# Causal attention and two gated layers in one kernel: the first batch's maxima over v emitted beside the first step, ordered behind its scores' minimum on VectorE

## The chip, the cores and the metric

The kernel runs on one core of a Trainium2 chip. The metric is the device time of one launch in microseconds (us); lower is better. Engines are TensorE (PE in the profile), VectorE (DVE), ScalarE (ACT), GpSimd (POOL) and SyncE (SP), which here only issues transfers.

## The reference

q, k, v have 4 batches, 8 heads, 576 positions and a head size of 64; s has one value for each position of each head.

```python
scores = scale * q @ k.T
cum = cumsum(maximum(s, 0), axis=-1)
bias = -(cum[..., :, None] - cum[..., None, :])
scores = where(causal, -1e9, scores + minimum(bias, 0))
attn = exp(scores - max(scores))
attn = attn / (sum(attn) + 1e-9)
x = (attn @ v) as 2304 tokens x 512
h = x @ w_in;   g = h * tanh(softplus(h));       x = g @ w_out      # 512 x 2048, 2048 x 512
h = x @ w_in2;  g = h * sigmoid(1.702 * h);      out = g @ w_out2   # 512 x 2048, 2048 x 512
```

q, k, v, s are float32; the four weight matrices are float64 and are turned into pairs of float32 parts on the chip.

## The kernel before

**Attention in steps.** A tile is 128 query rows of one batch (i = 0 to 4, the last with 64 rows); a group is a tile with four of the eight heads (g = 0, 1). A group is worked in one step (first tile), two steps (second tile) or more. Step t emits: `do_qk` (scores `s` on TensorE from `qw` and `kw`, into one of 4 PSUM banks of the pool `ps_s`), `do_max` (line 346, on VectorE: scores plus the row `ck` of running sums, with the minimum `mx`; the scores carry the opposite sign, so this minimum is the reference's maximum), `do_exp` (ScalarE), `do_hilo` (a scaled 16-bit part on ScalarE, line 372, the remainder on VectorE, line 373, both in `hl`, then one transposing load `pt` issued by SP, line 377). Four steps later (LAG = 4) `do_av` multiplies `pt` with v (lines 397 and 401, into `o`), and line 406 adds the parts.

**What feeds a step.** `load_group` fetches `kraw`, `qraw`, `vraw` of a group (`vraw` has three buffers); line 166 transposes k and q on TensorE into `kt` and `qt`; lines 174, 175, 188 and 189 split them into two parts each (`kw`, `qw`). `v1` and `v2` (lines 198, 202) split v into two 16-bit parts, scaled by `vs`, one number for a batch. `vs` comes from the largest absolute value of the batch's v: `vscale_load` fetches the whole v in three pieces `vl` of 128 x 768 (line 218), reduces each on VectorE (line 219) and joins them (line 222); `vscale_set` spreads the result (line 227), transposes it on TensorE (`vx`, line 229) and takes the reciprocal (lines 231 to 236). For the first batch `vscale_load(0)` is called in the setup, before `queue_prep(0)`, and `vscale_set(0)` by the first `v1` inside the first `tick`. For batches 1 to 3 both are queued at the second-last and last tile of the batch before.

**Buffers.** The pieces `vl` take buffers of the pool `mo_a` (five, tag `hs`), which the weights in conversion (`wst`) and the first layer's outputs (`hs`) use too.

**Order.** A planner gives every engine its instruction order: it plays the program through with its own durations, and an engine takes, of the instructions that are ready in that plan, the one that the program emitted first. The order is then fixed for each engine, and on the chip an engine waits at an instruction whose inputs are late. `add_manual_dep` with `order` adds an edge to the plan without a semaphore of its own. SP's transfers are issued in a fixed order as well.

**After the first two tiles** the first layer (`first_layer`, lines 581 to 583) runs among the attention's steps, as soon as 256 tokens are done; later the rest of both layers follows on TensorE.

Of the kernel before, what the change touches and what calls it, by code (L numbers as in the profile page):

```python
# [9 lines left out]
F32 = mybir.dt.float32  # L10
# [4 lines left out]
ALU = mybir.AluOpType  # L15
# [36 lines left out]
def attention_moe_moe_kernel(  # L52
# [12 lines left out]
    nc = tc.nc  # L65
# [41 lines left out]
    order = mybir.DependencyInfo(mybir.DependencyClass.NoSync, mybir.DependencyReason.DATA)  # L107
# [20 lines left out]
    def tmp_pair(dt, nm):  # L128
        tmp_n[0] += 1
        p = mo_a if mo_b[0] is None or tmp_n[0] % (MA + MBB) < MA else mo_b[0]  # L130
        return p.tile([128, 1024], dt, tag="hs", name=nm)
# [78 lines left out]
    VC = 3  # L210
    VW = H * S * D // 128 // VC

    def vscale_load(b):
        flat = v[b].rearrange("h t d -> (h t d)").rearrange("(p n) -> p n", p=128)
        vmx[b] = m = sm_p.tile([128, VC + 1], F32, tag="vm", name="vm")
        for c in range(VC):
            t = tmp_pair(F32, "vl")[:, 0:VW]
            nc.sync.dma_start(out=t, in_=flat[:, c * VW:(c + 1) * VW])
            nc.vector.tensor_reduce(
                out=m[:, c:c + 1], in_=t, axis=mybir.AxisListType.X, op=ALU.max, apply_absolute_value=True  # L220
            )
        nc.vector.tensor_reduce(out=m[:, VC:VC + 1], in_=m[:, 0:VC], axis=mybir.AxisListType.X, op=ALU.max)

    def vscale_set(b):
        m = vmx.pop(b)
# [25 lines left out]
    def load_ck(b, g):  # L251
        t = ck_p.tile([128, HG * LK], F32, tag=f"ck{g}", name=f"ck{g}").rearrange("p (h t) -> p h t", t=LK)
        ck[b, g] = t
        load_ck_part(b, g, 0, 128)
        if b:
            load_ck_part(b, g, 128, LK)
# [7 lines left out]
    def load_ckp(b, g):  # L264
        t = ck_p.tile([128, HG * LK], F32, tag=f"ck{g}", name=f"cp{g}")
        t = t[:, 0:HG // 2 * S].rearrange("p (h t) -> p h t", t=S)
        for a in range(2):
            h0 = g * HG + 2 * a
            nc.sync.dma_start(
                out=t[64 * a:64 * a + 64], in_=cum_d[b:b + 1, h0:h0 + 2, :].to_broadcast([64, 2, S])  # L270
            )
        ckp[b, g] = t
# [38 lines left out]
    def segs(x):  # L311
        if len(x["hs"][0]) == 1:
            return [(0, x["L"])]
        m = x["L"] // 2
        return [(0, m), (m, x["L"])]

    def do_qk(x):
        b, i, g, n, L = x["b"], x["i"], x["g"], x["n"], x["L"]
        x["S"] = []
        for c0, c1 in segs(x):  # L320
            ps = ps_s.tile([128, 512], F32, tag="s", name="s")
            x["S"].append(ps)
            for e, hs in enumerate(x["hs"]):
                o = ps[:, e * L:e * L + c1 - c0]
                for a, h in enumerate(hs):
                    hl = h - g * HG
                    for w in range(2):
                        nc.tensor.matmul(  # L328
                            out=o, lhsT=qw[b, i, g][:, hl, w, :], rhs=kw[b, g][:, hl, c0:c1],
                            start=(e == a == w == 0), stop=False, skip_group_check=True,  # L330
                        )
                if c1 == L:
                    nc.tensor.matmul(  # L333
                        out=o[:, c1 - c0 - n:c1 - c0], lhsT=identb, rhs=maskb if n == 128 else maskp,
                        start=False, stop=True, skip_group_check=True,
                    )

    def do_max(x):
        b, i, g, L = x["b"], x["i"], x["g"], x["L"]
        mx = sm_p.tile([128, HG], F32, tag="mx", name="mx")  # L340
        x["P"] = p = pp.tile([128, S], F32, tag="P", name="P", bufs=PB)
        for e, hs in enumerate(x["hs"]):
            hl = hs[0] - g * HG
            c = ckp[b, g][:, hl] if len(hs) == 2 else ck[b, g][:, hl]
            for f, (c0, c1) in enumerate(segs(x)):
                nc.vector.tensor_tensor_reduce(  # L346
                    out=p[:, e * L + c0:e * L + c1], in0=x["S"][f][:, e * L:e * L + c1 - c0], in1=c[:, c0:c1],
                    scale=1.0, scalar=mx[:, e:e + 1] if f else 3.0e38, op0=ALU.add, op1=ALU.min,
                    accum_out=mx[:, e:e + 1],
                )  # L350
        x["mx"] = mx

    def do_exp(x):
        ts = tile_state(x)
        L, p = x["L"], x["P"]
        for e in range(x["mu"]):
            o = p[:, e * L:(e + 1) * L]
            lut(
                o, o, AF.Exp, bias=x["mx"][:, e:e + 1], scale=-1.0,
                accum_out=ts["sums"][:, x["j"] + e, 0:1],  # L360
            )

    def do_hilo(x):
        L, mu, nb = x["L"], x["mu"], x["nb"]
        Lp = nb * 128
        w = mu * Lp
        hl = pp.tile([128, 2 * NTIL * 128], F16, tag="hl", name="hl", bufs=HLB)
        hv = hl[:, 0:2 * w].rearrange("p (a w) -> p a w", a=2)
        if Lp != L:
            nc.gpsimd.memset(hv[:, :, L:Lp], 0.0)  # L370
        wl = mu * L
        nc.scalar.activation(out=hv[:, 0, 0:wl], in_=x["P"][:, 0:wl], func=AF.Copy, scale=PSC)  # L372
        nc.vector.scalar_tensor_tensor(  # L373
            out=hv[:, 1, 0:wl], in0=x["P"][:, 0:wl], scalar=PSC, in1=hv[:, 0, 0:wl], op0=ALU.mult, op1=ALU.subtract
        )
        x["T"] = d = pt_p.tile([128, 2 * NTIL, 128], F16, tag="pt", name="pt")
        last_pt[0] = nc.sync.dma_start_transpose(out=d[:, 0:2 * mu * nb, :], in_=hl[:, 0:2 * w])
# [71 lines left out]
    late_k = {}  # L449

    VSTEP = {(3, 0): vscale_load, (4, 0): vscale_set}

    def queue_prep(gi):
        if gi >= len(groups):
            return
        b, i, g = groups[gi]
        items, vs, kT = split_items(b, i, g)
        if 0 < gi < len(groups) - 1:
            prep_q.append(lambda: load_group(*groups[gi + 1]))
        if i == 0 and b > 0:  # L460
            late_k[groups.index((b - 1, NTIL - 1, g))] = kT
        else:
            items = items + [kT]
        if gi < 2:
            v_first.extend(vs)
        else:
            items = items + vs
        if b + 1 < B and (i, g) in VSTEP:
            items = items + [lambda: VSTEP[i, g](b + 1)]
        prep_q.extend(items)  # L470

    def pop_prep(m):
        for _ in range(min(m, len(prep_q))):
            prep_q.pop(0)()
# [6 lines left out]
    def tick():  # L481
        t = nxt[0]
        nxt[0] += 1
        if t < NS:
            x = steps[t]
            gi = x["gi"]
            if first_of[gi] == t:
                pop_prep(len(prep_q))
                queue_prep(gi + 2)
            left = last_of[gi] - t + 1  # L490
            npop = -(-len(prep_q) // left)
        else:
            npop = len(prep_q)
        if t < NS:
            do_qk(x)
            do_max(x)
            do_exp(x)
            if last_of[gi] == t and gi in late_k:
                late_k.pop(gi)()
            if last_of[gi] == t and x["i"] == LK // 128 - 1:  # L500
                load_ckp(x["b"], x["g"])
            if last_of[gi] == t and x["i"] == NTIL - 1 and x["b"] + 1 < B:
                load_ck(x["b"] + 1, x["g"])
            do_hilo(x)
        if t == VT:
            for f in v_first:
                f()
        pop_prep(npop)
        while avn[0] < NS and t - avn[0] >= LAG:
            x = steps[avn[0]]  # L510
            do_av(x)
            if x["last"]:
                norm_tile(x)
                emit_q.append((t + (1 if avn[0] < ES else EDEL), x))
            avn[0] += 1
        while emit_q and emit_q[0][0] <= t:
            emit_tile(emit_q.pop(0)[1])
# [67 lines left out]
    def l1_mm(ps, lay, m, xr, first):  # L585
# [15 lines left out]
        out=maskb, in_=maskb, pattern=[[-1, 128]], compare_op=ALU.is_ge, fill=BIG, base=0, channel_multiplier=1  # L601
    )
    nc.gpsimd.memset(maskp, 0.0)
    for a in range(2):
        nc.gpsimd.affine_select(
            out=maskp[64 * a:64 * a + 64], in_=maskp[64 * a:64 * a + 64], pattern=[[-1, 64]],
# [138 lines left out]
    for m in range(NF):  # L745
        if m % 2 == 0:
            t = tmp_pair(F32, "hs")
# [5 lines left out]
        if m % 2:  # L753
            nc.sync.dma_start(
                out=h_d[:, m - 1:m + 1, (NU - UE) * U:NT], in_=t.rearrange("p (m t) -> p m t", m=2)
# [11 lines left out]
    for i, (u, t0, W, m0, n) in enumerate(groups1):  # L767
# [9 lines left out]
        for j in range(n):  # L777
            m = m0 + j
# [9 lines left out]
        if m0 + n == NF:  # L788
            k_ = 512 // W
            for e in range(KC * W // 512):  # L790
# [4 lines left out]
                for p in range(2):  # L795
                    nc.sync.dma_start(
                        out=x2_d[:, p, cs, t0:t0 + W],
                        in_=x2[:, p].bitcast(F32).rearrange("p (c t) -> p c t", c=k_),
# [105 lines left out]
```

## Time and profile before

| | |
|---|---|
| median of 3 runs | 1068.95 us (1063.43 to 1071.94) |
| profiled execution | 1066.92 us, of which the span is 1065.1 us |
| TensorE busy | 999.0 us, 94% of the span |
| VectorE busy | 557.4 us, 52% |
| ScalarE busy | 484.5 us, 45% |
| GpSimd busy | 273.3 us, 26% |

The span runs from the first to the last instruction; 1.8 us of the profiled execution lie outside it. Durations in the rows are those of this one execution. A transfer's issue on SP is not its landing; the time from the one to the other stands in the rows on transfers.

### The profile page before, as it was taken

To read this page: it belongs to the slowest core of one execution; us is meant where nothing else is said; L and a number is where in the kernel's file an instruction comes from. 1 tells how busy PE (TensorE), PEld (TensorE's weight loads), DVE (VectorE), ACT (ScalarE), POOL (GpSimd) and SP (SyncE) were. 2 spreads that over 40 slices of the span, in tenths; PEclk is the share of its full clock that TensorE was granted. 3 is DMA by queue.
4 is the path that set the end of the run, shared out by engine and by line. 5 is a ranking of instruction groups with operands and counts; after the bars stand their busy time and mean duration, and the time that the engine had idled before them with its cause. 6 is when DMAs were issued, how large, how long until landed. Compare 5 with 4: busy or idle time off the path is not lost.

```text
span 1065.1 us, 16948 instructions
## 1 busy us (share of the span) xinstructions
PE 999.0 (94%) x6396; PEld 865.6 (81%) x6396; DVE 557.4 (52%) x1074; ACT 484.5 (45%) x1010; POOL 273.3 (26%) x307
## 2 busy tenths in 40 slices
PE   3688899989999999999999979899999999999998
PEld 3577798888989889987888869688888888888897
DVE  5798786674557863576534575662222222222231
ACT  4778777584658862463212343442222222222121
POOL 3445532341124112655232254220000100100000
PEclk7679899989999999999999989899999999999999
DMA  9899987996699796797533656520300300210010
GB/s 231 161 251 277 258 208 172 231 188 161 139 222 219 146 196 198 251 382 276 178 119 119 194 166 195 158 80 6 114 1 0 99 20 1 60 40 1 20 40 20
DMA packets 192562, 154.35 MB, mean 145 GB/s; under 512 B 117921, under 2 KB 161953, under 8 KB 192481
## 3 DMA queue, kind: packets, MB, share of 16 engines
q1 hardware_dynamic: 182240, 131.25, 46.6%
q0 software_dynamic: 10240, 22.03, 8.1%
q8 instruction: 50, 0.82, 0.3%
q14 instruction: 32, 0.25, 0.1%
HBM read 93.92 MB, written 33.10 MB: 119 GB/s over the span
## 4 chain that ended last, share of the span: by engine, by line
PE 55%; DMA 10%; DVE 5%; POOL 3%; issue 2%; ACT 2%; SPq 0%; ACTq 0%; POOLq 0%; DVEq 0%
PE acc L844 18%; PE h L581 9%; PE h L582 9%; PE h L583 9%; DMA wst<-in_moe_w_out_dram 3%; DMA wst<-in_moe_w_in_dram 2%; POOL w L577 2%; PE s L328 2%; DVE wst L570 2%; PE acc L583 2%; PE acc L582 2%; PE acc L581 2%; DMA hg<-h_d 2%; DVE wst L566 1%; PE o L397 1%
## 5 line engine op out<-in xcount | busy, mean ns | idle before, releaser
L581 PE MATMUL h<-xh,w 128*128 128x256 f32 (+1 forms) x768 | 252.5, 331 | 8.5 <-DVE z L831 5.1
L582 PE MATMUL h<-xh,w 128*128 128x256 f32 (+1 forms) x768 | 248.4, 324 | 0.0
L583 PE MATMUL h<-xh,w 128*128 128x256 f32 (+1 forms) x768 | 246.9, 322 | 0.0
L844 PE MATMUL acc<-w,gh 128*128 128x512 f32 x576 | 177.8, 390 | 0.0
L581 PEld LDWEIGHTS h<-xh,w 128*128 128x128 f32 x768 | 147.6, 193 | 21.3 <-DVE z L831 5.5
L582 PEld LDWEIGHTS h<-xh,w 128*128 128x128 f32 x768 | 148.1, 193 | 10.8
L583 PEld LDWEIGHTS h<-xh,w 128*128 128x128 f32 x768 | 147.5, 192 | 10.5 <-POOL w L577 0.2
L831 DVE TENSOR_TENSOR z<-h,sg 128x512 f32<-128x512 f32 x72 | 49.7, 690 | 193.1 <-ACT sg L112 192.7
L112 ACT ACTIVATE sg<-h 128x512 f32<-128x512 f32 x72 | 42.9, 596 | 204.2 <-PE h L583 204.2
L844 PEld LDWEIGHTS acc<-w,gh 128*128 128x128 f32 x576 | 107.6, 188 | 21.7
L582 PE MATMUL acc<-gl,w 128*128 128x512 f32 (+1 forms) x320 | 120.1, 375 | 4.0 <-DVE gl L717 4.0
L581 PE MATMUL acc<-gh,w 128*128 128x512 f32 (+1 forms) x320 | 119.7, 374 | 3.1 <-POOL w L574 1.7
L577 POOL TENSOR_TENSOR w<-wst,w 128x512 fp32r<-128x512 f32 x64 | 90.6, 1418 | 116.7 <-ACT w L576 115.6
L583 PE MATMUL acc<-gh,w 128*128 128x512 f32 (+1 forms) x320 | 117.6, 374 | 0.7 <-POOL w L577 0.7
L844 PE MATMUL acc<-w,gl 128*128 128x512 f32 x288 | 112.2, 389 | 0.0
L112 ACT ACTIVATE P<-P,mx 128x128 f32<-128x128 f32 (+4 forms) x144 | 83.4, 580 | 33.0 <-DVE mx L346 32.1
L328 PE MATMUL s<-kw,qw 128*128 128x288 f32 (+4 forms) x384 | 90.0, 347 | 7.3 <-DVE kw L175 3.7
L373 DVE SCALAR_TENSOR_TENSOR hl<-P,hl 128x512 f16<-128x512 f32 (+2 forms) x104 | 73.1, 703 | 29.7 <-ACT hl L372 29.4
L809 POOL DMA_DIRECT2D xh<-x_d x20 | 14.5, 727 | 284.2 <-PE h L583 196.2
L833 DVE TENSOR_TENSOR gl<-z,gh 128x512 fp32r<-128x512 f32 x72 | 50.4, 701 | 49.4 <-ACT gh L832 34.9
L346 DVE CUSTOM_DVE_ANT_0 P<-s,ck 128x128 f32<-128x128 f32 (+3 forms) x128 | 59.3, 485 | 31.7 <-PE s L333 30.6
L582 PEld LDWEIGHTS acc<-gl,w 128*128 128x128 f32 x320 | 61.4, 192 | 15.1 <-DVE gl L717 4.8
(90 smaller groups left out, 1723.7 us busy)
## 6 DMA issues: line engine op xcount, KB each, us to landing
h_d<-hs SPq DMA_DIRECT2D x36, 512.0 KB, 4.6
hg<-h_d SPq DMA_DIRECT2D x36, 512.0 KB, 6.4
wst<-in_moe_w_in_dram SPq DMA_DIRECT2D x32, 512.0 KB, 4.8
wst<-in_moe_w_out_dram SPq DMA_DIRECT2D x32, 512.0 KB, 3.9
x_d<-x SPq DMA_DIRECT2D x36, 256.0 KB, 2.4
xh<-x_d POOLq DMA_DIRECT2D x16, 512.0 KB, 5.5
vl<-in_v_dram SPq DMA_DIRECT2D x12, 384.0 KB, 5.4
cp<-cum_d SPq DMA_DIRECT2D x16, 288.0 KB, 5.1
```

What stands on the lines that cost most here:

```text
L112: i = nc.scalar.activation(out=out, in_=in_, func=func, **kw)
L328: nc.tensor.matmul(out=o, lhsT=qw[b, i, g][:, hl, w, :], rhs=kw[b, g][:, hl, c0:c1], start=(e == a == w == 0), stop=False, skip_group_chec ...
L346: nc.vector.tensor_tensor_reduce(out=p[:, e * L + c0:e * L + c1], in0=x["S"][f][:, e * L:e * L + c1 - c0], in1=c[:, c0:c1], scale=1.0, sca ...
L373: nc.vector.scalar_tensor_tensor(out=hv[:, 1, 0:wl], in0=x["P"][:, 0:wl], scalar=PSC, in1=hv[:, 0, 0:wl], op0=ALU.mult, op1=ALU.subtract)
L570: nc.vector.scalar_tensor_tensor(out=yi, in0=yi, scalar=-(2 ** 31), in1=zi, op0=ALU.bitwise_and, op1=ALU.bitwise_or)
L577: nc.gpsimd.tensor_tensor(out=tl_, in0=y, in1=th, op=ALU.subtract)
L581: nc.tensor.matmul(out=outp, lhsT=hi_w, rhs=hi_x, start=start, stop=False, skip_group_check=True)
L582: nc.tensor.matmul(out=outp, lhsT=hi_w, rhs=lo_x, start=False, stop=False, skip_group_check=True)
L583: nc.tensor.matmul(out=outp, lhsT=lo_w, rhs=hi_x, start=False, stop=stop, skip_group_check=True)
L831: nc.vector.tensor_tensor(out=z, in0=ps, in1=sg, op=ALU.mult)
L833: nc.vector.tensor_tensor(out=gl, in0=z, in1=gh, op=ALU.subtract)
L844: nc.tensor.matmul(out=acc[tb], lhsT=gx[:, ts], rhs=w[:, wx, :], start=m == 0 and a == 0, stop=m == NF - 1 and a == 2, skip_group_check=True,)
```

## The change

`vscale_load` now takes its three buffers and asks for its three loads first, and puts the four reductions into a function `maxima`. For batches 1 to 3 it calls that at once. For the first batch it stores it in `v_late`, and the first `tick` calls it (VT = 0) after `do_hilo` of step 0 and before `v1` and `v2`; each of the three large reductions gets an order edge behind the last minimum instruction of step 0. The loads stay where they were. No instruction is added or removed.

```diff
     def vscale_load(b):
         flat = v[b].rearrange("h t d -> (h t d)").rearrange("(p n) -> p n", p=128)
         vmx[b] = m = sm_p.tile([128, VC + 1], F32, tag="vm", name="vm")
+        ts = [tmp_pair(F32, "vl")[:, 0:VW] for _ in range(VC)]
         for c in range(VC):
-            t = tmp_pair(F32, "vl")[:, 0:VW]
-            nc.sync.dma_start(out=t, in_=flat[:, c * VW:(c + 1) * VW])
-            nc.vector.tensor_reduce(
-                out=m[:, c:c + 1], in_=t, axis=mybir.AxisListType.X, op=ALU.max, apply_absolute_value=True
-            )
-        nc.vector.tensor_reduce(out=m[:, VC:VC + 1], in_=m[:, 0:VC], axis=mybir.AxisListType.X, op=ALU.max)
+            nc.sync.dma_start(out=ts[c], in_=flat[:, c * VW:(c + 1) * VW])
+
+        def maxima():
+            for c in range(VC):
+                r = nc.vector.tensor_reduce(
+                    out=m[:, c:c + 1], in_=ts[c], axis=mybir.AxisListType.X, op=ALU.max, apply_absolute_value=True
+                )
+                if b == 0:
+                    tc.add_manual_dep(r.ins, max_last[0].ins.name, order, reason="behind the first scores")
+            nc.vector.tensor_reduce(out=m[:, VC:VC + 1], in_=m[:, 0:VC], axis=mybir.AxisListType.X, op=ALU.max)
+
+        if b == 0:
+            v_late.append(maxima)
+        else:
+            maxima()
@@
+    max_last, v_late = [], []
+
     def do_max(x):
@@
-                nc.vector.tensor_tensor_reduce(
+                last = nc.vector.tensor_tensor_reduce(
@@
         x["mx"] = mx
+        max_last.append(last)
@@
         if t == VT:
+            v_late.pop()()
             for f in v_first:
                 f()
```

## Rows read from the trace of the kernel before

**Rows 1.** Busy time by stretch: TensorE, its loads, VectorE, ScalarE, GpSimd; granted clock; DMA share.
```profile
0.00:60.80 60.80, 31.51 (x194) 26.72 (x194) 43.15 (x105) 37.29 (x98) 26.34 (x45) 0.71 0.91 202
60.80:133.00 72.20, 62.83 (x535) 54.71 (x535) 61.46 (x148) 58.35 (x141) 38.87 (x43) 0.89 1.06 265
133.00:400.00 267.00, 257.04 (x2468) 234.88 (x2467) 177.38 (x470) 186.14 (x467) 71.26 (x100) 0.98 0.87 188
```

**Rows 2.** VectorE in order of time: start, duration, line, operation, idle time before it.
```profile
9.40 0.95 DVE L219 TENSOR_REDUCE vm<-vl 128x1 f32<-128x768 f32 x1 [0.88 <-DMA vl<-in_v_dram]
...
12.06 0.69 DVE L175 TENSOR_TENSOR kw<-kt,kw 64x512 fp32r<-64x512 f32 x1
12.78 0.95 DVE L219 TENSOR_REDUCE vm<-vl 128x1 f32<-128x768 f32 x1
13.76 0.29 DVE L346 CUSTOM_DVE_ANT_0 P<-s,ck 128x128 f32<-128x128 f32 x1
...
14.61 0.15 DVE L222 TENSOR_REDUCE vm<-vm 128x1 f32<-128x3 f32 x1
...
16.39 0.15 DVE L236 TENSOR_SCALAR vs<-vs 128x1 f32<-128x1 f32 x1
16.46 0.68 DVE L373 SCALAR_TENSOR_TENSOR hl<-P,hl 128x512 f16<-128x512 f32 x1
17.06 1.27 DVE L202 SCALAR_TENSOR_TENSOR v<-vraw,vs,v 128x256 f16<-128x256 f32 x3
```

**Rows 3.** Transfers issued in short stretches: bytes each and median us from issue to landing.
```profile
ck<-cum_d SPq DMA_DIRECT2D x1, 256.0 KB, 5.7
...
pt<-hl SPq DMA_TRANSPOSE x1, 9.0
```

**Rows 4.** ScalarE in order of time, columns as in rows 2.
```profile
14.10 0.40 ACT L112 ACTIVATE P<-P,mx 128x128 f32<-128x128 f32 x1 [4.60 <-DVE mx L346]
...
15.78 0.63 ACT L372 ACTIVATE hl<-P 128x512 f16<-128x512 f32 x1
...
26.44 0.51 ACT L198 ACTIVATE v<-vraw,vs 128x256 f16<-128x256 f32 x1 [3.36 <-DMA vraw<-in_v_dram]
27.99 0.60 ACT L188 ACTIVATE qw<-qt 128x512 fp32r<-128x512 f32 x1 [1.05 <-PE qt L166]
```

**Rows 5.** SP's issues in order of time: start and time taken to issue.
```profile
7.56 1.33 SPq L259 DMA_DIRECT2D ck<-cum_d  x2
17.17 4.11 SPq L377 DMA_TRANSPOSE pt<-hl  x1
21.38 0.52 SPq L142 DMA_DIRECT2D vraw<-in_v_dram  x1
```

**Rows 6.** TensorE in order of time, columns as in rows 2.
```profile
15.19 0.45 PE L229 MATMUL vx<-ident,vw 128*128 128x128 f32 x1 [5.07 <-DVE vw L227]
15.43 1.06 PE L166 MATMUL qt<-ident,qraw 128*128 128x128 f32 x4
...
26.23 0.29 PE L397 MATMUL o<-v,pt 128*128 128x128 f16 x1 [6.86 <-DMA pt<-hl]
26.86 1.10 PE L166 MATMUL qt<-ident,qraw 128*128 128x128 f32 x4
...
60.79 0.79 PE L581 MATMUL h<-xh,w 128*128 128x256 f32 x2 [0.85 <-ACT xh L442]
```

**Rows 7.** Busy time by stretch around the first transposed load, columns as in rows 1.
```profile
17.20:21.30 4.10, 2.17 (x13) 2.03 (x12) 3.36 (x13) 2.74 (x11) 2.85 (x4) 0.77 1.16 335
21.30:26.20 4.90, 0.00 (x0) 0.00 (x0) 1.31 (x3) 1.72 (x5) 0.80 (x2) 0.63 1.15 179
```

**Rows 8.** GpSimd in order of time: the copy of the fourth group's q.
```profile
22.29 0.40 POOL L148 COPY qraw<-qraw 128x256 f32<-128x256 f32 x1
```

**Rows 9.** Waits between 246 and 266 us: engine, line, released by, us in total, times, longest.
```profile
PE qt L166 <- DVE mx L346: 2.3, 1, 2.3
...
DVE vm L219 <- DMA vl<-in_v_dram: 2.4, 1, 2.4
```

## The prediction

> **What bounds the kernel now.** Read first the busy times by stretch [rows 1]. TensorE is the bound of the whole, but not of the place that is changed. In the first 60.8 us it works 31.5 us, so 29.3 us are idle there; from 60.8 to 133 us it idles 9.4 us, from 133 to 400 us 10.0 us. The first stretch is a chain of latencies that ends where the first layer starts, at 60.79 us [rows 6]. What is won or lost on that chain moves all that follows. What is won beside it is worth nothing.
>
> Next read VectorE, ScalarE, SP and TensorE side by side from 9 to 30 us. VectorE takes the three large reductions between the splits of q and k, the last of them from 12.78 us, and starts the first minimum at 13.76 us, straight behind it [rows 2]. That looks like a wait for a reduction, but the minimum needs the row `ck` as well: its first load was issued at 7.56 us [rows 5] and landed 5.7 us later [rows 3], at 13.26 us. So the reduction holds the minimum for at most about half a microsecond. ScalarE has stood idle for 4.60 us when the minimum comes [rows 4], so this half microsecond is on the path there. From there the path goes through four exponentials, the scaled part (15.78 to 16.41 us) [rows 4], the remainder on VectorE at 16.46 us [rows 2] and the transposing load at 17.17 us [rows 5].
>
> That load is where the path is decided. It lands 9.0 us after its issue [rows 3], and TensorE, which has run out of other work in its order, waits 6.86 us for it, to 26.23 us [rows 6]. ScalarE waits at the same time for the fourth group's v, up to 26.44 us [rows 4], which SP issued at 21.38 us, behind the 4.11 us that the issue of the transposing load took [rows 5]. In those 9 us the mean share of the 16 DMA engines is 1.16 and 1.15 [rows 7]: they have a backlog.
>
> **The change part by part.** Removed ahead of the first minimum: three reductions of 0.95 us. Without them VectorE has only the second group's splits of q and k there (that of k took 0.69 us) [rows 2], and these no longer queue behind a reduction. `ck` becomes the last to come. The minimum then starts at about 13.30 us (13.26 plus the 0.03 to 0.04 us that lay between neighbours before) in place of 13.76: 0.46 us earlier. The other bound is 0, if the planner leaves something else there.
>
> Added behind it: the three reductions, 0.98 us from the start of one to what followed it (12.78 to 13.76) [rows 2], 2.94 us together. The small join began at 14.61 us [rows 2]; now it begins at 14.61 - 0.46 + 2.94 = 17.09 us, 2.48 us later, and so do the spreading, the transpose `vx` on TensorE, the reciprocal and the split of v.
>
> Who waits for that? The split of v on VectorE began at 17.06 us and took 1.27 us for three groups [rows 2]; it would be 19.54 us, and 20.0 us when the first group's v is split. Its product comes at 26.23 us, and the buffer that it frees is wanted by SP only at 21.38 us [rows 5]. That covers it with 1.4 us to spare; without the long issue of 4.11 us SP would wait for v here.
>
> The remainder of step 0 is the second one that can be held. It becomes ready at 16.46 - 0.46 = 16.00 us. The reductions would occupy VectorE from 14.15 to 17.09 us, the third from 16.11 us. If the planner puts the remainder ahead of the third, the transposing load is issued at 16.71 us, 0.46 us earlier; if it comes behind all three, it starts at 17.09, 0.63 us later than now. No row shows which. I take the first, since the program emits the remainder ahead of the reductions, and keep -0.46 and +0.63 as bounds.
>
> TensorE: `vx` stood right ahead of the third group's transposes (15.19 and 15.43 us) [rows 6]. Were the order kept, these and step 1's scores would slip by 2.48 us, to 17.9 us. Behind them TensorE idles 6.86 us [rows 6], which covers it. If `vx` is planned behind them, nothing slips.
>
> The loads for v stay in place. For batches 1 to 3 the same seven operations are emitted in another order, loads first. How SP's order changes there no row tells. One such load cost something before: VectorE waited 2.4 us for it, and TensorE 2.3 us in turn [rows 9]. That bounds the effect for a batch at -2.3 to +2.3 us; I take 0, since no instruction is added and the first of the three reductions still has the same load to wait for.
>
> How much of 0.46 us reaches 26.23 us? Each transfer carries its latency along, as the 9.0 us row says if taken as it stands [rows 3]: all of it. That is my sum: 0.46 us less, 1066.92 - 0.46 = 1066.46 us for the profiled execution. The median of the three runs lies 2.03 us above that execution, so 1068.5 us. With the rule of the Trainium skill, DMA: Bandwidth & Descriptors, section Queues, rings and completion order, the sum would be another: each DMA engine takes turns between the queue rows that have work, a packet at a time, so what is issued earlier into full engines shares them with the same neighbours. By that rule the sum is 0, the first rival below; that the engines are full is what the trace shows, that they take turns no row shows.
>
> **The rivals.**
>
> *The backlog sets the landing.* The DMA engines are full from 17.2 to 26.2 us [rows 7], and the bytes ahead of the transposing load don't change. Then it lands at 26.2 us whenever it is issued within half a microsecond, and both bounds above (-0.46, +0.63) shrink to 0: 1068.95 us. For it speaks the 4.11 us that the issue itself took [rows 5]; against it nothing but that the share is a mean over 16 engines. An edge that the planner ignores, so that the reductions stay in place, would give the same time.
>
> *The product is planned later (faster).* TensorE's order has step 0's product ahead of the fourth group's transposes, which then start at 26.86 us [rows 6], though their copy was ready at 22.69 us [rows 8]. In the plan v now comes 2.48 us later, so the product may be planned behind them. ScalarE takes that group's v ahead of its q, at 26.44 us [rows 4]; if that stays, q's split comes at 26.95 in place of 27.99 us, a gain of 1.0 us; if that flips too, up to 26.86 - 22.69 = 4.2 us. So 1064.8 to 1067.9 us, most likely some 1067.5.
>
> *The remainder queued behind the scale (slower).* If the planner puts the remainder of step 0 not only behind the reductions but behind the reciprocal chain, as it stands now (the last of that chain at 16.39, the remainder at 16.46 us) [rows 2], VectorE reaches it 2.48 us later, in order. The transposing load is then issued 2.5 us later, and the fourth group's v with it; TensorE and ScalarE, who both wait for these, move from 26.2 to 28.7 us: 1071.4 us. It decides from the point where the remainder is planned later than `vs`. Against it: by the durations above the remainder is ready 1.1 us ahead of the join, and `vx` has still to come after that.
>
> *The plan comes out otherwise further on.* The planner's near ties can flip down to 400 us. What is at stake is the 19.4 us that TensorE idles from 60.8 to 400 us [rows 1], in pieces like the 2.3 us [rows 9]. A few of them gone or new is 3 to 8 us either way: 1061 to 1066, or 1072 to 1077 us. It takes more than half of these 19.4 us, gone or added, to reach 1%.
>
> **How the numbers follow.** Forecast, 0.46 us off: 0.30. Backlog (or an edge without effect): 0.23. Product later, faster by 1 to 4 us: 0.15. Remainder behind the scale: 0.10. Another plan further on: 0.12 faster, 0.10 slower. The likeliest gives 1068.5 us. One per cent is 10.7 us, about what a measurement of this kernel can tell from no change, as its three runs spread over 8.5 us; only the last case can reach it, with some half of its chance: 0.07 faster, 0.06 slower, 0.87 within. The range takes the runs' own spread (1063.4 to 1071.9), the slower rival on top of its upper part and a piece of the last case on each side: 1060.5 to 1076.
>
> **What would show it right or wrong.** Right: no reduction ahead of the first minimum; the minimum at about 13.3 us, held by the landing of `ck`; the transposing load issued near 16.7 us and landing near 25.7; the first layer starting within 1 us of 60.79 us. Landing still at 26.2 speaks for the backlog; the fourth group's transposes before the first product for the faster rival; the remainder's start past 18.9 us for the slower one. Wrong in the whole: a start of the first layer moved by more than 3 us, or idle time of TensorE between 60.8 and 400 us changed by more than 5 us.

## The result and the profile after

The changed kernel takes 1073.91 us (median of 20 runs, 1064.88 to 1079.01) against 1067.59 us for the kernel before on the same chips (20 runs, 1061.59 to 1075.12). The ratio is 1.0063 with an interval of 1.0043 to 1.0082, so the change costs some 6.5 us. The forecast was 1068.5 us, half a microsecond faster. The profiled execution of the changed kernel took 1074.98 us with a span of 1073.2 us, 8.1 us longer than the span of before.

The first place to look is the one that was edited. VectorE of the changed kernel in order of time, as in [rows 2]:

```profile
13.17 0.29 DVE L358 CUSTOM_DVE_ANT_0 P<-s,ck 128x128 f32<-128x128 f32 x1 [2.96 <-DMA ck<-cum_d]
...
14.02 2.67 DVE L222 TENSOR_REDUCE vm<-vl 128x1 f32<-128x768 f32 x3
16.61 0.68 DVE L386 SCALAR_TENSOR_TENSOR hl<-P,hl 128x512 f16<-128x512 f32 x1
17.21 0.15 DVE L227 TENSOR_REDUCE vm<-vm 128x1 f32<-128x3 f32 x1
...
19.50 0.88 DVE L202 SCALAR_TENSOR_TENSOR v<-vraw,vs,v 128x256 f16<-128x256 f32 x2 [0.39 <-ACT v L198]
```

The reductions are gone from ahead of the first minimum, which now waits for `ck` (2.96 us) and starts 0.59 us earlier. They stand behind it, and the remainder of step 0 behind them. The answers to [rows 5], SP's issues, are these:

```profile
17.48 4.23 SPq L390 DMA_TRANSPOSE pt<-hl  x1
21.81 0.52 SPq L142 DMA_DIRECT2D vraw<-in_v_dram  x1
```

to [rows 3], the transfers issued in short stretches:

```profile
ck<-cum_d SPq DMA_DIRECT2D x2, 256.0 KB, 5.9
...
pt<-hl SPq DMA_TRANSPOSE x1, 7.1
```

and to [rows 6], TensorE in order of time:

```profile
17.76 0.45 PE L239 MATMUL vx<-ident,vw 128*128 128x128 f32 x1 [6.70 <-DVE vw L237]
...
24.66 0.29 PE L410 MATMUL o<-v,pt 128*128 128x128 f16 x1 [3.07 <-DMA pt<-hl]
...
61.11 0.80 PE L595 MATMUL h<-xh,w 128*128 128x256 f32 x2
```

The transposing load is issued 0.31 us later than before and lands 1.9 us sooner after its issue; `vx` and what follows it slip by 2.57 us and are swallowed by TensorE's idle time, 6.86 us before and 3.07 us now. The first layer starts 0.32 us later than before. Nothing of 8.1 us is lost here. The busy times by stretch, columns as in [rows 1], say where it is:

```profile
0.00:60.80 60.80, 32.59 (x197) 28.15 (x198) 41.66 (x105) 36.98 (x97) 26.21 (x45) 0.81 0.84 199
60.80:133.00 72.20, 58.29 (x511) 50.24 (x508) 60.06 (x131) 53.96 (x125) 39.08 (x42) 0.90 1.09 256
133.00:400.00 267.00, 251.89 (x2382) 229.65 (x2383) 178.11 (x481) 185.72 (x477) 70.51 (x99) 0.98 0.89 185
```

From 60.8 to 400 us TensorE idles 72.20 - 58.29 + 267.00 - 251.89 = 29.0 us, where it idled 72.20 - 62.83 + 267.00 - 257.04 = 19.3 us before [rows 1] (the prediction's 19.4 is the sum of two rounded parts). That stretch runs code that the diff does not touch. What differs there is the order of the instructions: the planner, given one more order edge, puts 289 of TensorE's 6396 instructions in other places, 144 of VectorE's 914, 130 of ScalarE's 865, 22 of GpSimd's 307 and 6 of SP's 354 (the expectations of the later runs count a little fewer, since there two instructions of the same kind count as one). In the kernel before the last of them run at 153 us on TensorE, 157 us on VectorE and 163 us on ScalarE; from there the two orders are the same. The edge alone does it: with the reductions emitted late but without it, the order is that of before.

### The profile page after: what moved, and what is told of

It reads as the page before. It is cut to its first block, busy times and chain, and to the rows that moved or that the text cites. A ratio compares the mean times of both kernels' runs of the same rounds, so it can differ in the third digit from the quotient of the medians.

```text
span 1073.2 us, 16941 instructions
## 1 busy us (share of the span) xinstructions
PE 995.8 (93%) x6396; PEld 862.5 (80%) x6396; DVE 560.7 (52%) x1074; ACT 483.8 (45%) x1010; POOL 275.1 (26%) x307
## 4 chain that ended last, share of the span: by engine, by line
PE 53%; DMA 10%; DVE 5%; POOL 4%; issue 4%; ACT 2%; SPq 0%; POOLq 0%; ACTq 0%; DVEq 0%
PE acc L858 18%; PE h L595 8%; PE h L596 8%; PE h L597 8%; DMA wst<-in_moe_w_out_dram 3%; PE acc L596 2%; PE acc L597 2%; PE acc L595 2%; DMA wst<-in_moe_w_in_dram 2%; POOL w L591 2%; DMA pt<-hl 1%; PE s L338 1%; DVE wst L584 1%; DMA x_d<-x 1%; DVE gl L731 1%
## 5 line engine op out<-in xcount | busy, mean ns | idle before, releaser
L595 PE MATMUL acc<-gh,w 128*128 128x512 f32 (+1 forms) x320 | 118.4, 370 | 2.5 <-POOL w L588 1.5
L597 PE MATMUL acc<-gh,w 128*128 128x512 f32 (+1 forms) x320 | 116.2, 370 | 0.7 <-POOL w L591 0.7
L386 DVE SCALAR_TENSOR_TENSOR hl<-P,hl 128x512 f16<-128x512 f32 (+2 forms) x104 | 75.7, 730 | 27.9 <-ACT hl L385 27.1
L578 ACT ACTIVATE wst<-wst 128x512 f32<-128x512 f32 x48 | 32.9, 685 | 88.9 <-DMA wst<-in_moe_w_out_dram 47.6
```

Source lines behind the costliest of these rows:

```text
L386: nc.vector.scalar_tensor_tensor(out=hv[:, 1, 0:wl], in0=x["P"][:, 0:wl], scalar=PSC, in1=hv[:, 0, 0:wl], op0=ALU.mult, op1=ALU.subtract)
L578: nc.scalar.activation(out=y, in_=y, func=AF.Copy, scale=2.0 ** -112)
L595: nc.tensor.matmul(out=outp, lhsT=hi_w, rhs=hi_x, start=start, stop=False, skip_group_check=True)
L597: nc.tensor.matmul(out=outp, lhsT=lo_w, rhs=hi_x, start=False, stop=stop, skip_group_check=True)
```

## The experiments

All but e7 have each engine's order written out by hand, as a chain of order edges over the list of emitted instructions:

```diff
+    if PLAN:
+        made = list(nc.cur_bb.bb.instructions)
+        for line in PLAN:
+            for i0, i1 in zip(line, line[1:]):
+                tc.add_manual_dep(made[i1], made[i0].name, order, reason="plan")
```

So an order can be exchanged between the two kernels engine by engine, or up to a point in time. Below, B is the order of the kernel before and A that of the changed kernel. All ratios are to the kernel before, timed beside them; they are given as recorded, with their 95% intervals, and are not quite the quotient of the two medians; e1 to e4 shared a chip and runs, as did e5 to e7, e8 to e11, e12 to e15 and e16 to e18.

### Place or order (e1, e2)

```diff
 e1: PLAN = A -> B on all engines; on VectorE the three reductions
     behind the first minimum, step 0's remainder right behind them
 e2: PLAN = A on all engines, the three reductions where B has them
```

> The kernel's order is pinned on all five engines: everywhere the order of the kernel before, only the three large reductions stand behind the first minimum on VectorE, with the remainder of step 0 right behind them. Order theory (the loss comes from the other order that the planner made of the rest, up to 150 us): 0 to 1 us from before, first layer's start within 1 us of 60.8 us, no long stall of TensorE near 130 us. Place theory (the late scale itself costs, on the chip): about the whole loss, 5 to 7 us slower than before.

> The counterpart: the three reductions stand where they stood before, ahead of the first minimum, and every other instruction of all engines is pinned in the order of the changed kernel. Order theory: as slow as the changed kernel, 5 to 7 us over before, with TensorE's stall of some 7 us near 130 us. Place theory: as before, within 1 us.

e1 took 1066.64 us against 1066.81, 1.0000 (0.9970 to 1.0031); e2 1073.00 us, 1.0070 (1.0045 to 1.0095). The theory of the place, 5 to 7 us slower, falls: the maxima can stand behind the first minimum at no cost that can be read. The interval is some 3 us wide on either side, so the 0.46 us that the prediction forecast can be neither confirmed nor refuted by it. The theory of the order holds: with the maxima back in their old place, the other order costs all of it. e1 also shows that writing an order out by hand costs nothing that can be read.

### Which stretch (e3, e4, e14, e15)

```diff
 e3:  PLAN = A up to the first layer's first matmul (61 us), then B
 e4:  PLAN = B up to there, then A
 e14: PLAN = A up to TensorE's place 500 (about 100 us), then B
 e15: PLAN = B up to there, then A
```

> The changed kernel's order up to the first matmul of the first layer (about 61 us), from there on the order of the kernel before. Order theory: within 1 us of before, since the changed kernel was only 0.4 us late at 61 us. Place theory (the late first steps leave something that is paid later, whatever the order): 5 to 7 us slower.

> The order of the kernel before up to the first matmul of the first layer, reductions ahead of the first minimum, then the changed kernel's order. Order theory: 5 to 7 us slower than before, the loss between 85 and 140 us. Place theory: as before, within 1 us.

> The changed kernel's order on every engine up to TensorE's place 500 (about 100 us), then the order of the kernel before. If the loss is made between the first layer's start at 61 us and 100 us, where the changed kernel's profile shows TensorE waits of 1.5 and 1.8 us and a granted clock of 0.50, 1.005 or more; if at the change of batches behind 100 us, 1.001 as the cut at 61 us; if both have a part, about 1.003.

> The opposite cut: the order of the kernel before up to about 100 us, then the changed kernel's. Loss made ahead of 100 us: 1.000 to 1.001. Loss made at the change of batches: 1.004 to 1.0055. Both: about 1.003.

A up to 61 us: 1.0012 (0.9980 to 1.0044). A from 61 us: 1.0040 (1.0009 to 1.0070). A up to 100 us: 1.0008 (0.9979 to 1.0037). A from 100 us: 1.0018 (0.9992 to 1.0044). Most of the loss is made behind 61 us, but a cut at 100 us leaves neither half with it. The expectation of e14 and e15, that one stretch or the other has it, was not met: what costs the time seems to stand on both sides of 100 us, with less in each half than can be read, or it comes only where both halves have A's order; no run tells these two apart.

### One stall that looked guilty (e5, e6)

The longest wait of TensorE in the changed kernel's profile is at the change of batches. In order of time, one line each from ScalarE, VectorE and TensorE:

```profile
135.49 0.42 ACT L150 ACTIVATE qraw<-qraw 128x256 f32<-128x256 f32 x1 [4.24 <-DMA qraw<-in_q_dram]
135.81 0.58 ACT L188 ACTIVATE qw<-qt 128x512 fp32r<-128x512 f32 x1
...
136.42 0.69 DVE L189 SCALAR_TENSOR_TENSOR qw<-qt,qw 128x512 fp32r<-128x512 f32 x1 [8.20 <-ACT qw L188]
...
137.17 1.11 PE L443 MATMUL xt<-ident,x 128*128 128x128 f32 x4 [7.29 <-DVE qw L189]
```

Read from below: TensorE waits 7.29 us for VectorE, which has waited 8.20 us for the first half of a split q, which ScalarE can't make because the copy of another q tile stands ahead of it in its order and waits for its load. In B that copy stands behind the split. e5 and e6 exchange this piece alone:

```diff
 e5: PLAN = A, but ScalarE's places 176 to 191 as in B
 e6: PLAN = B, but ScalarE's places 176 to 191 as in A
```

> The changed kernel, its order pinned on all engines, with one stretch of 16 ScalarE instructions near 125 us put in the order of the kernel before: the duplicating copies of the next group's q and k stand behind the split of the present q and its exponentials, not ahead of them. Blocked-copy theory (ScalarE waits in order for a late load of q, so that the split behind it keeps a PSUM bank and TensorE stands 7.3 us): that stall shrinks to under 2.5 us and the kernel is within 0 to 3 us of before. Many-places theory (the loss is spread over the whole other order): still 5 us or more slower than before.

> The counterpart: the kernel before, pinned, with only that stretch of 16 ScalarE instructions in the changed kernel's order. Blocked-copy theory: a stall of TensorE of 4 to 7 us near 128 us and 3 to 6 us slower than before. Many-places theory: within 1.5 us of before.

e5 took 1072.59 us, 1.0071 (1.0044 to 1.0098), e6 1.0009 (0.9987 to 1.0031). The theory, that ScalarE's order of these 16 is what costs, fell. In e5's profile the same TensorE instruction waits 0.41 us:

```profile
128.22 1.11 PE L468 MATMUL xt<-ident,x 128*128 128x128 f32 x4 [0.41 <-DVE qw L198]
```

and that execution took 1066.44 us, but the median of e5's runs is as late as ever. The profiled execution is the fastest of e5's seven, so its profile can't tell what the median paid; how long this stall was in the other six is not known. What e5 and e6 show is that the order of these 16 ScalarE instructions is neither needed for the loss nor enough for it. The last part of this section comes back to the stall from VectorE's side.

### Any other order (e7)

```diff
-    for g in range(2):
+    for g in (1, 0):
```

in the loading of `ck`, nothing written out by hand: the planner then gives a third order, 319 places on TensorE away from B.

> The kernel before with only the first two loads of the running sums emitted in the other order (second four heads first), no order pinned: same work, another plan (319 of TensorE's 6396 places differ), in which the copy of the late q stands one place behind the split and not ahead of it. If any other plan costs what the changed kernel's did (the tuned order was lucky): 3 to 8 us slower than before. If the cost hangs on that copy ahead of the split: within 3 us of before, though step 0 itself may start about 0.6 us later, with its row of sums loaded second.

It took 1067.12 us against 1066.31, 1.0021 (0.9998 to 1.0045). Another order does not cost 0.65% as such.

### Which engine (e8 to e13, e16 to e18)

```diff
 e8:  PLAN = A, but GpSimd and SyncE as in B
 e9:  PLAN = B, but GpSimd and SyncE as in A
 e10: PLAN = A, but TensorE as in B
 e11: PLAN = B, but TensorE as in A
 e12: PLAN = B, but VectorE and ScalarE as in A
 e13: PLAN = A, but VectorE and ScalarE as in B
 e16: PLAN = B, but ScalarE as in A without its places 102 to 112
 e17: PLAN = B, but VectorE as in A
 e18: PLAN = B, but ScalarE's places 102 to 112 and VectorE's 118 to 129 as in A
```

In e9, e11, e12, e16, e17 and e18 the reductions stay where B has them; in e8, e10 and e13 they stand behind the first minimum.

> The changed kernel's order on TensorE, VectorE and ScalarE, but the order of the kernel before on the two engines that issue the loads (SyncE and GpSimd: 6 of 354 and 22 of 307 places go back). If the order in which the loads are issued costs the 0.65%, this kernel stands at 1.000 of the kernel before; if the order on the compute engines costs it, at 1.0065 (some 1073.5 us against 1067); if each has a part, between the two, about 1.003.

> The opposite: the kernel before with only the changed kernel's order on SyncE and GpSimd. Theory of the load queues: 1.0065. Theory of the compute order: 1.000, within the 0.3% of the interval. Parts on both sides: about 1.003.

> The changed kernel's order everywhere but on TensorE, which keeps the order of the kernel before (277 of 6396 places go back). If TensorE's order costs it (a product stands ahead of work whose operands are ready), 1.000; if not, 1.0065. A third outcome is a loss above 1.0065: the engines' orders then fit only one another, and TensorE waits for operands that the others make later.

> The opposite: the kernel before with only the changed kernel's order on TensorE. TensorE's order costs it: 1.0065. Another engine's order costs it: 1.000. Orders that fit only one another: above 1.0065, as the run with the opposite exchange.

> The kernel before with the changed kernel's order on VectorE and ScalarE alone (132 of 914 and 127 of 865 places; the reductions stay ahead of the first minimum). If these two engines' order is the part that costs, 1.005 to 1.0065; if parts add up (0.23% measured for the load queues alone), about 1.003 to 1.004; if it needs the load queues as well, 1.000.

> The opposite: the changed kernel with VectorE's and ScalarE's order of the kernel before, the reductions still behind the first minimum. These engines' order costs it: 1.000 to 1.0015. Parts that add up: 1.002 to 1.003, as the load queues alone. The load queues cost it: 1.0065.

> The kernel before with the changed kernel's order on ScalarE alone, but for 11 places (102 to 112 of 865, at about 105 us) that can't stand without VectorE's order. If ScalarE's order costs it, 1.005 to 1.0065; if VectorE's, or if those 11 places are the cause, 1.000; if both engines have a part, about 1.003.

> The kernel before with the changed kernel's order on VectorE alone (132 of 914 places; the reductions stay ahead of the first minimum). VectorE's order costs it: 1.005 to 1.0065. ScalarE's order costs it: 1.000. Both have a part: about 1.003. If only the two together cost it, 1.000 here and in the run with ScalarE's order.

> The kernel before with one block of the changed kernel's order: ScalarE's places 102 to 112 and VectorE's 118 to 129, where the first halves and remainders of two q tiles (qw) go ahead of a raw copy, an exponential, v and a remainder of P. If this block is the cause, 1.005 to 1.0065; if not, 1.000.

| run | engines in A's order | ratio | interval |
|---|---|---|---|
| e8 | TensorE, VectorE, ScalarE | 1.0027 | 0.9992 to 1.0062 |
| e9 | GpSimd, SyncE | 1.0023 | 0.9990 to 1.0057 |
| e10 | all but TensorE | 1.0053 | 1.0024 to 1.0082 |
| e11 | TensorE | 1.0006 | 0.9976 to 1.0035 |
| e12 | VectorE, ScalarE | 1.0064 | 1.0034 to 1.0094 |
| e13 | TensorE, GpSimd, SyncE | 0.9997 | 0.9974 to 1.0020 |
| e16 | ScalarE, but 11 places | 1.0026 | 0.9995 to 1.0056 |
| e17 | VectorE | 1.0078 | 1.0047 to 1.0108 |
| e18 | one block at 105 us on both | 1.0000 | 0.9975 to 1.0025 |

VectorE's order alone brings the whole loss (e17), and A without VectorE's and ScalarE's order is as fast as before (e13), load queues and all. TensorE's own order is nothing (e11). e8 is the one run that fits badly: it has VectorE's order and reads only 1.0027; its interval reaches to 1.0062, so it doesn't contradict e17, but it leaves room for a part of the load queues. Its executions fall apart, eight from 1062.3 to 1069.6 us and the others from 1075.2 us on. ScalarE's order by itself can't be told from nothing (e16). Over all runs, the seven kernels with the whole of A's order on VectorE, the reductions apart (after, e2, e5, e8, e10, e12, e17), read 1.0027 to 1.0078, with a mean of 1.0061; the six with the whole of B's (e1, e6, e9, e11, e13, e16) read 0.9997 to 1.0026, with a mean of 1.0010. The one block that ties the two engines' orders together is not it (e18); the traces put it at 80 to 86 us, not at the 105 us of the expectation.

The idle time of TensorE in the profiles points the same way, though one execution each is a weak witness. The two later stretches of [rows 1] for e17, e12 and e13:

```profile
60.80:133.00 72.20, 59.78 (x512) 51.24 (x511) 58.54 (x132) 54.90 (x127) 37.46 (x42) 0.90 1.09 256
133.00:400.00 267.00, 255.75 (x2397) 233.89 (x2398) 178.61 (x483) 188.38 (x478) 72.43 (x101) 0.97 0.84 185
```

```profile
60.80:133.00 72.20, 57.08 (x503) 49.68 (x502) 56.49 (x138) 52.40 (x125) 34.99 (x39) 0.88 1.03 250
133.00:400.00 267.00, 253.82 (x2398) 232.23 (x2397) 177.78 (x471) 186.74 (x472) 72.73 (x100) 0.98 0.85 183
```

```profile
60.80:133.00 72.20, 62.66 (x519) 54.19 (x517) 57.40 (x144) 55.10 (x135) 36.70 (x40) 0.86 1.08 254
133.00:400.00 267.00, 257.75 (x2503) 235.42 (x2501) 177.21 (x470) 186.54 (x468) 72.14 (x100) 0.99 0.86 188
```

Idle in the two stretches: 23.7 us in e17, 28.3 in e12, 18.8 in e13, against 19.3 before. Not every profile fits: e9, with B's order on VectorE, idles 25.8 us there, and e5, with A's, 20.2 us.

### What VectorE's order does

With VectorE known, its two orders were read side by side. The change of batches comes back, now seen from the other engine. The kernel before, VectorE in order of time (the reading of the accumulators and three like minima left out):

```profile
124.77 0.69 DVE L175 TENSOR_TENSOR kw<-kt,kw 64x512 fp32r<-64x512 f32 x1
125.50 0.29 DVE L346 CUSTOM_DVE_ANT_0 P<-s,ck 128x128 f32<-128x128 f32 x1
...
126.69 0.42 DVE L346 CUSTOM_DVE_ANT_0 P<-s,ck 128x256 f32<-128x256 f32 x1
...
128.95 0.69 DVE L189 SCALAR_TENSOR_TENSOR qw<-qt,qw 128x512 fp32r<-128x512 f32 x1 [1.83 <-ACT qw L188]
```

e17, with A on VectorE alone:

```profile
129.16 0.69 DVE L184 TENSOR_TENSOR kw<-kt,kw 64x512 fp32r<-64x512 f32 x1
132.60 0.69 DVE L198 SCALAR_TENSOR_TENSOR qw<-qt,qw 128x512 fp32r<-128x512 f32 x1 [2.74 <-ACT qw L197]
133.21 0.28 DVE L383 CUSTOM_DVE_ANT_0 P<-s,ck 128x128 f32<-128x128 f32 x1
```

In B, six minima over scores that are ready stand between a split of k and the remainder of a q tile. In A the remainder of q stands ahead of the six. It needs the first half from ScalarE, which needs a transposed copy, which needs a load that was issued a few microseconds ago. The six minima stand behind it in VectorE's order, so they wait for that load too (133.21 us in e17, 125.50 before); behind them wait their exponentials, and the scores' buffers come free later. In the changed kernel the remainder comes at 136.42 us (the row above, 8.20 us of idle time), and TensorE pays 7.29 us at once.

Every profile has one or the other. Between the end of the split of k and the first of the six minima lie 0.03 us in all ten kernels that have B here (before, e1, e3, e6, e9, e11, e13, e14, e16, e18), and 8.8, 5.0, 6.2, 2.9, 2.8, 4.7, 6.3, 8.8, 5.2 and 3.4 us in the ten that have the remainder of q ahead (after, e2, e4, e5, e7, e8, e10, e12, e15, e17). The ratios measured for the first ten, the kernel before left out, lie from 0.9997 to 1.0026, with a mean of 1.0009; those of the second ten from 1.0018 to 1.0078, with a mean of 1.0051. Over the 20 profiles the delay and the span go together with a correlation of 0.73. e5 fits in: with ScalarE's order put back the six minima still wait behind the remainder (2.9 us in its profile), and it still costs.

Why TensorE pays can be read from the programs: the planner hands out the four PSUM banks of `ps_s` along with the order. In the ten kernels that have the remainder ahead of the minima, TensorE's next transposes `xt` get the bank of that very q (`qt`) and must wait for its remainder; in the ten others they get another bank. Their wait in the profiles is 0.4 to 7.3 us in the first ten, 2.9 us on average, and nothing in the others. So the exchange of VectorE's order was an exchange of banks as well: in e17, 35 of the 224 tiles of `ps_s` lie in other banks than before, in the same as in the changed kernel. The six kernels with B's order on VectorE have B's banks. No run separates the order from the banks.

So the exchange shows that VectorE's order, with the banks that go with it, brings the loss. That this one instruction, six places early, is the cause is argued and not shown: it was not tried by itself, and three things speak against its being the whole. e7 and e15 have it and read only 1.0021 and 1.0018, not to be told from nothing; the interval of e15 ends at 1.0044, and that of e17 begins at 1.0047. The size of the loss isn't that of the delay (e17 has 3.4 us and the largest ratio). And in e17's profile TensorE loses next to nothing at this place. The transposes `xt` of the kernel before, and those of e17:

```profile
129.08 1.06 PE L430 MATMUL xt<-ident,x 128*128 128x128 f32 x4
```

```profile
133.35 1.11 PE L468 MATMUL xt<-ident,x 128*128 128x128 f32 x4 [0.41 <-DVE qw L198]
```

They come 4.3 us later than before, but the split of k ahead of the remainder was 4.4 us late already (129.16 and 124.77 us). In the changed kernel the split is 2.8 us late (127.53 us) and `xt` 8.1 us (137.17 us). Other places of VectorE's order, the banks, or a small part of the load queues (e8, e9) may bring the rest; that stays open.

## Why the prediction was wrong

Most steps around the edited place came out nearly as written.

- The minimum: 13.17 us, held by `ck`; forecast 13.30.
- The reductions: three in 14.02 to 16.61, 2.59 us; forecast 2.94. The term was a little too large: back to back the three take 2.67 us together, where one alone took 0.95 [rows 2].
- The join at 17.21 us (forecast 17.09), `vx` at 17.76 (2.48 us later than 15.19 is 17.67), the split of v at 19.50 (forecast 19.54), all covered by TensorE's idle time as written.
- The remainder of step 0: the bound, not the value taken. It came behind all three reductions, at 16.61, 0.15 us later than before (the bound was 0.63), and the transposing load was issued 0.31 us later instead of 0.46 earlier.
- The landing: neither "each transfer carries its latency along" nor a fixed landing at 26.2 us. It was issued later and its product began at 24.66 us, sooner by 1.57. The rule that was weighed there (the Trainium skill, DMA: Bandwidth & Descriptors, section Queues, rings and completion order: engines take turns between queues that have work) doesn't give a landing time by itself, and this trace doesn't show the fixed one that was drawn from it.
- The first layer: within 1 us, as the text asked (60.79 and 61.11 us). e1 shows that the change in its place, B's order kept, is worth nothing that can be read (1.0000, 0.9970 to 1.0031).

The step that failed is the sum's silent one: that beyond the first product the kernel runs in the order of before, so that no term stands for what comes behind that; a plan that comes out otherwise had only 0.22 of the chance, as a rival. The rival "The plan comes out otherwise further on" is what happened, on its slower side: it was priced at 3 to 8 us from TensorE's 19.4 us of idle time [rows 1], and 9.7 us were added to those in the profiled execution; its sign of being right, idle time changed by more than 5 us between 60.8 and 400 us, is there. Mechanism and size stood in the text with a chance of 0.10, and the measured 1073.91 us lies inside the stated range only because that was widened, on its upper side, for the slower rivals. Whether the 0.46 us of the likeliest case were gained can't be read from any of the medians. The sentence "the planner's near ties can flip" was too weak: an order edge on three reductions that end at 17 us changed 591 places in the queues of five engines, up to 163 us; e2 shows that this order alone costs the whole (1.0070), and e17 that VectorE's part of it does (1.0078). The reorder of the loads for batches 1 to 3, which was bounded at 2.3 us, changes no place at all.

That a loss at 60 to 150 us reaches the end is seen further on. The split of the expert weights resumes on GpSimd at 413.77 us in the kernel before and at 421.85 us in the changed one, 8.1 us later (the waits in brackets are alike):

```profile
413.77 0.76 POOL L574 TENSOR_SCALAR w<-wst 128x512 fp32r<-128x512 f32 x1 [9.37 <-DVE wst L570]
```

```profile
421.85 0.76 POOL L588 TENSOR_SCALAR w<-wst 128x512 fp32r<-128x512 f32 x1 [9.54 <-DVE wst L584]
```

From there the chain that ends last runs through those weights for long stretches (with TensorE's own work in between, from 490 to 552 us). The changed kernel's chain in order of time:

```profile
662.41 2.92 POOL w L591 x2
665.35 4.54 DMA wst<-in_moe_w_out_dram
669.96 0.68 ACT wst L578
670.67 0.71 DVE wst L580
671.40 1.73 DVE wst L584
...
675.27 4.20 DMA wst<-in_moe_w_out_dram
...
681.61 0.80 PE h L595
```

A load of 4 to 5 us, a pass each on ScalarE, VectorE and GpSimd, and the buffer for the next load. TensorE has slack against it: it waits until 674.07 us before and until 681.61 us after, 7.5 us later. TensorE itself comes to this wait only 3.5 us late (it waits 5.11 us before and 9.14 us after), so its slack has taken up some of the delay; the weights, which started late, have not, and they decide when it goes on.

## What to carry to other kernels

An edit to a kernel whose order a planner makes is two edits: the one in the diff, and a new order everywhere that the planner's times reach. Price the second from the idle time of the bounding engine in the stretches behind the edit, give it a chance of its own size, and, if the edit is meant to be local, write the rest of the order out by hand and compare.

Exchange the orders between the two kernels engine by engine and in both directions before reading causes off a trace: the longest stall stood in the first profile, but which engine's order brings the loss only the exchange told. Look at what goes with an order, too: here the planner's buffers changed with it.

Look for ready work that stands, in an engine's order, behind work that hangs on a load just issued: here one remainder of 0.69 us held six ready minima for 3 to 9 us. What that costs the kernel by itself was not measured.

## What was not expected of the hardware

The first transposing load, in almost the same place in every kernel, took from 5.4 us (e14) to 9.6 us (e16) between its issue and the first product, over 20 profiles. The 0.46 us on which the forecast turned is about a tenth of this spread of 4.2 us. And TensorE's granted clock differs by stretch, between its two levels of 1.2 and 2.4 GHz: from 84 to 100 us its mean is 0.68 in the changed kernel, with 11.63 us of work in 16, where the kernel before has 0.89 with 14.02 us:

```profile
84.00:100.00 16.00, 11.63 (x79) 10.08 (x78) 12.30 (x26) 10.67 (x25) 6.52 (x6) 0.68 1.13 268
```

```profile
84.00:100.00 16.00, 14.02 (x113) 12.06 (x112) 13.47 (x33) 13.53 (x31) 8.79 (x10) 0.89 1.12 311
```

The changed kernel (the first row) did 79 matmuls there against 113, so a part of what is lost in these 16 us is slower work and not waiting; how much, no run separates. Over the whole stretch from 60.8 to 133 us the clock is alike, 0.90 after and 0.89 before, so it is no ready explanation of the 6 us.
